# Strided-and-local attention with a squared-ReLU MLP: matmul slots of the two layers grouped by fours (by threes in the second chunk), with one head's scores ahead of the ups and one head's outputs ahead of the downs

## The chip, the cores and the metric

The kernel runs on one core of one Trainium2 chip. The metric is the device time of one execution in microseconds (us). The kernel before takes 880.53 us (median of 3 runs, 880.10 to 881.49).

## What is computed

```python
def _attn_ref(q, k, v):                       # 8 batches, 8 heads, 576 positions, 64 per head
    scores = scale * np.matmul(q, k.transpose(0, 1, 3, 2))
    rel = pos[:, None] - pos[None, :]
    mask_local = (rel >= 0) & (rel < 32)
    mask_strided = (rel >= 0) & (pos[None, :] % 32 == pos[:, None] % 32)
    # heads 0 to 3 use mask_local, heads 4 to 7 mask_strided
    attn = softmax(np.where(mask, scores, -1e9))
    return np.matmul(attn, v)

def _moe_ref(x, w_in, w_out):                 # x: 4608 tokens x 512, w_in 512 x 2048, w_out 2048 x 512
    h = np.maximum(x @ w_in, 0.0)
    return h * h @ w_out
```

The attention output of all heads, laid side by side, is the `x` of the second function. All data are float32.

## The kernel before

**Chunks and slots.** The 4608 tokens are cut into 12 chunks (`NCHUNK`) of 384 tokens (`TC`). The MLP of one chunk is 16 slots (`NFT`), one for each 128 columns of the inner dimension. Every number is split into a high and a low part, so each product is three matmuls. `up(c, j)` (L466) is the first layer of slot j: 12 matmuls of 384 columns into one PSUM bank (`psum` 0, 1 or 2, in turn), then ReLU and square on ScalarE (L487, L488; in the first chunk ReLU on ScalarE and the square on VectorE), the high part `gh` (ScalarE, L489) and the low part `gl` (VectorE, L490). `gh` and `gl` have two buffers each. `down(c, j)` (L494) is the second layer of the slot: 9 matmuls of 512 columns, three for each of the three 128-token tiles `y` of the chunk, which sum up in three banks of their own over all 16 slots. After slot 15 the three tiles are copied to `ysb` (L513) and stored (L514), all on SyncE's queue.

**Attention of the next chunk, beside the MLP of this one.** The strided heads (`strided`, L400) run on GpSimd (products, L426 and L448) and VectorE (sums over them, L427 and L449) and write `xsh`/`xsl` (L459, L460). The local heads of the first two chunks are computed in pairs (`pe_pair`, L295), those of the third and later ones (`NPLAIN`) one at a time by the generator `pe_head` (L199). It has six steps: the two loads on SyncE's queue (L214, L215), the high and low parts of q and k (L220 to L223), the four score matmuls (L237) with mask and minimum on VectorE, the softmax (L246 to L254), the transposes and `px` (L257 to L272), the four output matmuls (L283) with the writing of `xlh`/`xll` (L290, L291). Chunk c+1 has 4 such heads, 40 in all.

**What orders the work.** The framework schedules the instructions of each engine by a simulation, earlier-written ones first where several are ready; `tc.issue_after(ins)` adds that what is written in its block follows `ins` on the same engine. On TensorE this is a hand-written order: `last["pe"]` is the last instruction placed, and `take` (L580) puts the next step of a head behind it. In the first chunk (L657 to L664) ups and downs are free against each other, and the weights, loaded and split into high and low parts by `convert` (L147), come in beside them. From the second chunk on the loop (L655) goes by pairs of slots: two ups, then the two downs of the pair before. So the downs run two slots behind, and the last pair's downs of a chunk come after the first two ups of the next chunk. The table `plan` (L569) says for each of the 8 pairs which heads take a step ahead of the ups, between ups and downs, and after them: scores stand between in pairs 0 and 1 and ahead of the ups in pairs 4 and 5; outputs stand between in pairs 2 and 3 and ahead of the ups in pairs 6 and 7. The strided steps are spread over the slots by `SPREAD` and a cost count (L690 to L710).

Of the kernel before, what the change touches and what calls it, by code (L numbers as in the profile page):

```python
# [18 lines left out]
STR = 32  # L19
# [26 lines left out]
WRATE = 2  # L46

# [39 lines left out]
def attn_moe(ctx: ExitStack, tc, qk_l, v_l, qk_d, v_d, qk_p, v_p, f_s, q_s, k_s, v_s, w_in, w_out, masks, eye, out):  # L87
# [4 lines left out]
    xpool = pool("xpool", 2)  # L92
    gpool = pool("gpool", 2)
    ypool = pool("ypool", 3)
# [4 lines left out]
    ps_y = pool("ps_y", NTT, space=PSUM)  # L99
    ps = pool("ps", 1, space=PSUM)  # L100

    def psum(i, nm):
# [96 lines left out]
    def pe_head(c, h):  # L199
# [95 lines left out]
    def pe_pair(c, pr, local, qk, vr, es, pt, banks, sm, single):  # L295
# [67 lines left out]
        yield  # L363
        p4 = pt.rearrange("p (h w q) -> p h w q", h=2, w=NW)
        for h in range(2):
            t = s_ps[h] if s_ps else banks()

            for w in [*range(NW)] * (2 if c == 0 and local and not pr and h else 1):
                nc.tensor.transpose(t[:kw, w * QC : (w + 1) * QC], e4[h][:, w], ident[:QC, :QC])  # L369
            if c == 0 and not local:  # L370
                nc.vector.tensor_copy(pt[:kw, h * TC : (h + 1) * TC], t[:kw, :TC])
            else:
                last["a"] = nc.scalar.copy(pt[:kw, h * TC : (h + 1) * TC], t[:kw, :TC])
        yield
        x = x_tiles(c)
        if local:
            o = s_ps[0] if s_ps else banks()

            for w in [*range(NW)] * (3 if c == 0 and not pr else 1):
                for h in range(2):  # L380
                    nc.tensor.matmul(o[D * h : D * (h + 1), w * QC : (w + 1) * QC], v4[:kw, h, w], p4[:kw, h, w], start=True, stop=True)  # L381
            outs = [(o[:, :TC], [x["l", s][:, pr, :] for s in "hl"])]
        else:
# [3 lines left out]
            for a in range(2):  # L387
                o = s_ps[a]
                for w in range(NW):
                    for h in range(2):  # L390
                        p0 = r0 + STR * h
                        nc.tensor.matmul(o[p0 : p0 + STR, w * QC : (w + 1) * QC], v4[:kw, h, w, STR * a : STR * (a + 1)], p4[:kw, h, w], start=True, stop=True)
                by_i = lambda t: t[r0 : r0 + D].rearrange("p (s i r) -> p s i r", s=2, r=STR)
# [72 lines left out]
    def up(c, j):  # L466
# [4 lines left out]
        for kt in range(4):  # L471
# [3 lines left out]
            for w, xx in ((wi[p][0], xh), (wi[p][0], xl), (wi[p][1], xh)):  # L475
                done = nc.tensor.matmul(ph[:, :TC], w[:, wsl], xx, start=n == 0, stop=n == 11)  # L476
# [16 lines left out]

    def down(c, j):  # L494
        gh, gl = g_tiles.pop((c, j))
        p, o = divmod(j, 2)
# [8 lines left out]
        wsl = slice(o * DM, (o + 1) * DM)  # L505
        for t in range(NTT):
            sl = slice(t * P, (t + 1) * P)
            for k, (g, w) in enumerate(((gh, wo[p][0]), (gh, wo[p][1]), (gl, wo[p][0]))):
                done = nc.tensor.matmul(y_ps[c][t], g[:, sl], w[:, wsl], start=j == 0 and k == 0, stop=j == NFT - 1 and k == 2)  # L509
        if j == NFT - 1:  # L510
            for t in range(NTT):
                y = ypool.tile([P, DM], F32, name=f"ysb{c}_{t}", tag="ysb")
                (nc.scalar.copy if t == 1 else nc.vector.tensor_copy)(y, y_ps[c][t])  # L513
                nc.sync.dma_start(out=out[c * TC + t * P : c * TC + (t + 1) * P, :], in_=y)  # L514
        return done
# [17 lines left out]


    def pair_at(c, pr, local, place, psum_at):
        u = f"{c}_{pr}_{int(local)}"
        buf = lambda pl, nm, n, tag, **kw: pl.tile([P, n], F32, name=f"{nm}{u}", tag=tag, **kw)
        ee = lambda pl, tag: [buf(pl, f"e{h}", 512, tag) for h in range(2)]
        if place == 0:
            b = buf(lraw, "qk", TC + KC, "qk"), buf(lpool, "v", 512, "vx", bufs=1), ee(lpool, "e"), buf(lpool, "pt", 2 * TC, "px")  # L540
        elif place == 1:
            b = buf(lraw, "qk", TC + KC, "qk"), buf(ypool, "v", 512, "ysb"), ee(ypool, "ysb"), buf(lpool, "pt", 2 * TC, "px")
        elif place == 2:
            e = buf(xpool, "e", 2 * TC, "xlh")
            b = buf(xpool, "qk", 2 * TC, "xll"), buf(xpool, "v", 2 * TC, "xsl")[:, :512], [e[:, :TC], e[:, TC:]], buf(lpool, "pt", 2 * KC, "kx", bufs=1)[:, : 2 * TC]
        else:

            t = buf(wpool, "w", 2048, "w7")
            b = buf(xpool, "qk", 2 * TC, "xsh"), buf(spool, "v", 512, "s3", bufs=5), [t[:, :512], t[:, 512:1024]], t[:, 1024 : 1024 + 2 * TC]
        it = iter(range(10))  # L550
# [9 lines left out]
    def local(c):  # L560
# [7 lines left out]
    heads = {}  # L568
    plan = {  # L569
        0: ("", "0", "01"),  # L570
        1: ("", "1", "012"),
        2: ("", "0", "123"),
        3: ("", "1", ""),
        4: ("2", "", "23"),
        5: ("3", "", "23"),
        6: ("2", "", "3"),
        7: ("3", "", ""),
    }
# [74 lines left out]

    NS = NCHUNK * NFT
    for s in range(NS + 2):  # L655
        c, j = divmod(s, NFT)
        if s < NFT:  # L657

            with ExitStack() as seq:
                if s:  # L660
                    seq.enter_context(tc.issue_after(last["up"].ins))
                last["up"] = up(c, j)
            if s >= 2:
                last["pe"] = down(*divmod(s - 2, NFT))  # L664

        elif s % 2 == 0:
            before, between, rest = plan[j // 2]
            for part, slots, two in (up, (s, s + 1), before), (down, (s - 2, s - 1), between):
                take(c + 1, two)
                with tc.issue_after(last["pe"].ins):  # L670
                    for i in slots:
                        if 0 <= i < NS:
                            last["mm"] = part(*divmod(i, NFT))
                last["pe"] = last["mm"]
            take(c + 1, rest)
        if s < NFT - 2:

            weights = behind({"a": last["gh"]} | ({"x": last["xs"]} if s > NFT - 4 else {}), ungated)
            for _ in range(WRATE):
                next(weights, "end")  # L680
            weights_end = {e: last[e] for e in "agsv"}
        if s == LATER:
            zbank = (4,)
        if s == NFT - 1:
            with tc.issue_after(weights_end["g"].ins):
                for t in p_t:
                    nc.gpsimd.memset(t, 0.0)
        if j == NFT - 2:
            take(c + 2, "010")
        if c + 1 < NCHUNK and s >= LATER:  # L690
            j0 = LATER if c == 0 else 0
# [16 lines left out]
            if j == NFT - 1:  # L708
                run(lo)
                run(st)  # L710


# [74 lines left out]
```

## Time and profile before

| | |
|---|---|
| median of 3 runs | 880.53 us (880.10, 880.53, 881.49) |
| span of the profiled execution, first to last instruction | 877.8 us; no other time is listed for it |
| VectorE, ScalarE, GpSimd busy | 640.3, 571.4, 672.2 us (73%, 65%, 77%) |
| instructions | 14,934 |

The span is 2.7 us under the median: the rest lies before the first and after the last instruction. In the rows of the profile PE is TensorE's matmuls, PEld its weight loads, DVE VectorE, ACT ScalarE, POOL GpSimd, SPq SyncE's queue. A row of the chain of waits gives start, length and work; a row of the groups gives busy time and mean ns of one after the bar, then the idle time before it and what ended it. In a row of instructions in order of time, the start and the length come first, and an idle time before it stands in brackets. Matmuls overlap in the records: one of 512 columns is listed with 0.39 us and the next starts 0.23 us after it.

### The profile page before, as it was taken

What the parts mean: (1) busy time and instruction counts of PE and PEld (TensorE: products, weight loads), DVE (VectorE), ACT (ScalarE), POOL (GpSimd) and SP (SyncE); (2) the same over time, 40 slices, a digit from 0 to 9 for tenths busy, and PEclk for the clock granted to TensorE, in tenths of its full rate; (3) what the DMA queues carried; (4) which work ended last, traced back from release to release, by engine and by line L of the source; (5) the groups of instructions that cost most, each with busy time, mean ns of one, the idle gap of its engine ahead of it and who ended that gap; (6) DMA issues with size and microseconds to landing.
All of it is one profiled execution on the core that took longest, in us unless ns stands there. A gap on an engine that the chain in (4) does not pass through costs nothing.

```text
span 877.8 us, 14934 instructions
## 1 busy us (share of the span) xinstructions
PE 867.9 (99%) x4787; PEld 788.9 (90%) x4787; DVE 640.3 (73%) x1900; ACT 571.4 (65%) x1506; POOL 672.2 (77%) x718
## 2 busy tenths in 40 slices
PE   8999999999999999999999999999999999999997
PEld 7788899999999999999989898989898989999996
DVE  5796587797787887878878779878778787883111
ACT  6998776586576666657756758657666665664332
POOL 3689778877978989888988978996998899782000
PEclk9999999999999999999999999999999999999999
DMA  9963531223123023112102302312031021000000
GB/s 351 363 212 95 178 95 46 85 84 114 32 86 103 27 89 103 44 62 87 58 9 80 116 13 77 100 32 75 31 103 58 29 71 62 7 0 15 23 1 37
DMA packets 26799, 71.42 MB, mean 81 GB/s; under 512 B 2976, under 2 KB 8736, under 8 KB 25184
## 3 DMA queue, kind: packets, MB, share of 16 engines
q1 hardware_dynamic: 26432, 70.14, 24.1%
q8 instruction: 38, 0.62, 0.3%
q14 instruction: 41, 0.34, 0.1%
q10 hardware_dynamic: 288, 0.33, 0.1%
HBM read 61.01 MB, written 9.44 MB: 80 GB/s over the span
## 4 chain that ended last, share of the span: by engine, by line
PE 95%; ACT 2%; POOL 1%; issue 0%; DVE 0%; DVEq 0%; POOLq 0%; ACTq 0%
PE h L476 45%; PE y L509 45%; PE s L237 2%; PE o L283 2%; ACT b L353 1%; PE w_ps L606 1%; PE b L325 1%; POOL w L173 1%; ACT raw L154 0%; ACT z L166 0%; POOL pq L426 0%; ACT w L172 0%; PE b L381 0%; ACT xsh L396 0%; PE b L369 0%
## 5 line engine op out<-in xcount | busy, mean ns | idle before, releaser
L509 PE MATMUL y<-w,gh 128*128 128x512 f32 x1152 | 357.9, 391 | 0.5 <-POOL w L173 0.5
L509 PEld LDWEIGHTS y<-w,gh 128*128 128x128 f32 x1152 | 212.7, 188 | 40.5 <-POOL w L173 0.8
L476 PE MATMUL h<-xlh,w 128*128 128x384 f32 x768 | 229.1, 339 | 1.3 <-ACT xlh L396 0.6
L448 POOL TENSOR_TENSOR pp<-vs,sc 128x448 f32<-128x448 f32 (+10 forms) x192 | 190.0, 1014 | 48.8 <-DVE qs L449 23.0
L476 PE MATMUL h<-xsh,w 128*128 128x384 f32 x768 | 226.4, 335 | 0.3 <-POOL w L173 0.3
L509 PE MATMUL y<-w,gl 128*128 128x512 f32 x576 | 225.2, 392 | 0.0
L426 POOL TENSOR_TENSOR pq<-ks,qs 128x512 f32<-128x512 f32 (+2 forms) x192 | 197.7, 1050 | 18.8 <-DVE sc L427 13.3
L490 DVE TENSOR_TENSOR gl<-h,gh 128x384 fp32r<-128x384 f32 x192 | 105.5, 550 | 80.9 <-ACT gh L489 79.8
L489 ACT CAST gh<-h 128x384 fp32r<-128x384 f32 x192 | 91.8, 478 | 104.3 <-PE y L509 103.3
L487 ACT ACTIVATE h<-h 128x384 f32<-128x384 f32 x176 | 83.1, 472 | 109.8 <-PE h L476 109.3
L427 DVE TENSOR_REDUCE sc<-pq 128x8 f32<-128x512 f32 (+4 forms) x228 | 119.7, 534 | 45.1 <-POOL pq L426 41.9
L476 PEld LDWEIGHTS h<-xlh,w 128*128 128x128 f32 x768 | 141.3, 188 | 4.9 <-ACT w L172 0.9
L476 PEld LDWEIGHTS h<-xsh,w 128*128 128x128 f32 x768 | 141.3, 188 | 1.1 <-POOL w L173 0.6
L476 PE MATMUL h<-xll,w 128*128 128x384 f32 x384 | 129.0, 336 | 0.0
L509 PEld LDWEIGHTS y<-w,gl 128*128 128x128 f32 x576 | 108.1, 188 | 22.9
L476 PE MATMUL h<-xsl,w 128*128 128x384 f32 x384 | 128.4, 334 | 0.0
L449 DVE TENSOR_REDUCE qs<-pp 128x64 f32<-128x448 f32 (+11 forms) x192 | 106.4, 562 | 27.3 <-POOL pp L448 25.5
L488 ACT ACTIVATE h<-h 128x384 f32<-128x384 f32 x176 | 83.3, 473 | 3.6
L262 DVE STREAM_TRANSPOSE p_t<-e 32x128 f32<-32x128 f32 x240 | 72.3, 301 | 11.2 <-ACT e L251 6.6
L476 PEld LDWEIGHTS h<-xll,w 128*128 128x128 f32 x384 | 72.2, 188 | 2.4 <-DVE xll L397 0.3
L476 PEld LDWEIGHTS h<-xsl,w 128*128 128x128 f32 x384 | 72.1, 188 | 0.2
L246 ACT ACTIVATE e<-e,nm 96x128 f32<-96x128 f32 x160 | 62.5, 392 | 10.1 <-DVE nm L229 8.7
(101 smaller groups left out, 1076.7 us busy)
## 6 DMA issues: line engine op xcount, KB each, us to landing
qk<-qk_l SPq DMA_DIRECT2D x24, 400.0 KB, 3.2
y<-ysb SPq DMA_DIRECT2D x36, 256.0 KB, 3.5
raw<-w_in SPq DMA_DIRECT2D x7, 1024.0 KB, 10.9
qk<-qk_l SPq DMA_DIRECT2D x16, 416.0 KB, 3.6
vs<-v_s SPq DMA_DIRECT2D x10, 576.0 KB, 3.9
raw<-w_out SPq DMA_DIRECT2D x5, 1024.0 KB, 12.6
v<-v_l SPq DMA_DIRECT2D x40, 128.0 KB, 2.1
ks<-k_s SPq DMA_DIRECT2D x8, 576.0 KB, 3.8
```

The costliest lines, as they stand in the source:

```text
L246: nc.scalar.activation(e[:QC, cut(w)], e[:QC, cut(w)], AF.Exp, bias=nmax[:QC, w : w + 1], scale=-1.0, accum_out=ssum[:QC, w, :1])
L262: nc.vector.transpose(out=pt[STR * k : STR * (k + 1), :, STR * r : STR * (r + 1)], in_=e.rearrange("p (w k) -> p w k", k=KW)[STR * r : STR ...
L426: nc.gpsimd.tensor_mul(pv, kt[:, a : a + m, :], qt[:, i - i0 : i - i0 + 1, :].broadcast_to([P, m, D]))
L427: nc.vector.tensor_reduce(out=sc[:, i - i0, a : a + m], in_=pv, op=ALU.add, axis=AX.X)
L448: nc.gpsimd.tensor_mul(pv, vt[:, a : a + nd, :n], sc[:, il : il + 1, :n].broadcast_to([P, nd, n]))
L449: nc.vector.tensor_reduce(out=ot[:, il, a : a + nd], in_=pv, op=ALU.add, axis=AX.X)
L476: done = nc.tensor.matmul(ph[:, :TC], w[:, wsl], xx, start=n == 0, stop=n == 11)
L487: nc.scalar.activation(g, g, AF.Relu)
L488: nc.scalar.activation(g, g, AF.Square)
L489: last["gh"] = nc.scalar.copy(gh, g)
L490: nc.vector.tensor_sub(gl, g, f32(gh))
L509: done = nc.tensor.matmul(y_ps[c][t], g[:, sl], w[:, wsl], start=j == 0 and k == 0, stop=j == NFT - 1 and k == 2)
```

## The change

Chunks from the second on are cut into groups of slots: 3, 3, 3, 3, 4 in the second chunk (`GROUPS`), four fours in the later ones. A group is all its ups, then all its own downs, so downs no longer trail by a pair, and the first chunk's last two downs come ahead of the second chunk's first up. `plan` is gone. With n the running number of the group, head n has its scores ahead of the ups of group n and its outputs ahead of the downs of group n+1; a new `yield` makes `px` a step of its own, taken ahead of the ups of group n+1. A head's loads are asked for at the end of group n-2.

The buffers of `gh` and `gl` go from two to three pairs (two are used in the first chunk). For it `px` goes from two buffers to one, and the second pair of local heads of the first chunks keeps its transposed scores in the third pair of `g`; the transposed scores become two tiles, one for each head.

In the last group of the last chunk the downs of slot 12 come first, then those of slots 13 to 15 tile by tile. The last tile is copied out in halves by VectorE and ScalarE, and each half is stored by a queue of its own (SyncE's and ScalarE's).

```diff
+GROUPS = (3, 3, 3, 3, 4), (4, 4, 4, 4)
...
-    gpool = pool("gpool", 2)
+    gpool = pool("gpool", 1)
...
+    g_pair = lambda i, dtype=F32R: [gpool.tile([P, TC], dtype, name=f"g{i}{k}", tag=f"g{i}{k}") for k in "hl"]
...
+        yield
         src = pt.rearrange("p w q -> p (w q)")
-        px = lpool.tile([P, 2, TC], F32R, name=f"px{u}", tag="px")
+        px = lpool.tile([P, 2, TC], F32R, name=f"px{u}", tag="px", bufs=1)
...
-        gh = gpool.tile([P, TC], F32R, name=f"gh{c}_{j}", tag="gh")
-        gl = gpool.tile([P, TC], F32R, name=f"gl{c}_{j}", tag="gl")
+        gh, gl = g_pair(j % 2 if c == 0 else (c * NFT + j) % 3)
...
-    def down(c, j):
+    def down(c, j, tiles=range(NTT)):
...
+                if c == NCHUNK - 1 and t == NTT - 1:
+                    half = slice(0, DM // 2), slice(DM // 2, DM)
+                    nc.vector.tensor_copy(y[:, half[0]], y_ps[c][t][:, half[0]])
+                    nc.scalar.copy(y[:, half[1]], y_ps[c][t][:, half[1]])
+                    nc.sync.dma_start(out=rows[:, half[0]], in_=y[:, half[0]])
+                    nc.scalar.dma_start(out=rows[:, half[1]], in_=y[:, half[1]])
...
+    def on_pe(parts):
+
+        with tc.issue_after(last["pe"].ins):
+            for part, *which in parts:
+                pe = part(*which)
+        last["pe"] = pe
...
+            for i in (NFT - 2, NFT - 1):
+                on_pe([(down, 0, i)])
...
+    def head(n):
+
+        if n >= 0:
+            take(NPLAIN + n // HL, (n % HL,))
+
+    n = 0
+    for c in range(1, NCHUNK):
+        j = 0
+        for size in GROUPS[min(c, 2) - 1]:
+            slots = range(j, j + size)
+            head(n)
+            head(n - 1)
+            on_pe([(up, c, i) for i in slots])
+            head(n)
+            head(n - 1)
+            for i in slots[: size // 2]:
+                pace(c, i)
+            if slots[-1] == NFT - 1 and c == NCHUNK - 1:
+                on_pe([(down, c, slots[0])])
+                for t in range(NTT):
+                    on_pe([(down, c, i, (t,)) for i in slots[1:]])
+            else:
+                on_pe([(down, c, i) for i in slots])
+            for i in slots[size // 2 :]:
+                pace(c, i)
+            head(n)
+            head(n + 1)
+            head(n + 2)
+            n += 1
+            j += size
```

More of the change, by code (lines that the diff above doesn't have):

```diff
@@ L363, in pe_pair @@
         yield
[L364 removed]
+        p3 = [t.rearrange("p (w q) -> p w q", w=NW) for t in pt]
         for h in range(2):
@@ L492, in up @@
         return done
-    def down(c, j):
-        gh, gl = g_tiles.pop((c, j))
+    def down(c, j, tiles=range(NTT)):
+        gh, gl = g_tiles.pop((c, j)) if tiles[-1] == NTT - 1 else g_tiles[c, j]
         p, o = divmod(j, 2)
@@ L505, in down @@
         wsl = slice(o * DM, (o + 1) * DM)
-        for t in range(NTT):
+        for t in tiles:
             sl = slice(t * P, (t + 1) * P)
@@ L652, in attn_moe, with pace @@
     zbank = (3, 4)
[L654 to L690, printed above, removed]
+    def pace(c, j):
+        nonlocal lo, st, dl, ds, cost
+        if c + 1 < NCHUNK and (c or j >= LATER):
             j0 = LATER if c == 0 else 0
@@ L710, in attn_moe @@
                 run(st)
+    lo = st = dl = ds = cost = None
+    for j in range(NFT):
+        with ExitStack() as seq:
+            if j:
+                seq.enter_context(tc.issue_after(last["up"].ins))
+            last["up"] = up(0, j)
+        if j >= 2:
+            last["pe"] = down(0, j - 2)
+        if j < NFT - 2:
+            weights = behind({"a": last["gh"]} | ({"x": last["xs"]} if j > NFT - 4 else {}), ungated)
+            for _ in range(WRATE):
+                next(weights, "end")
+            weights_end = {e: last[e] for e in "agsv"}
+        if j == LATER:
+            zbank = (4,)
+        if j == NFT - 1:
+            with tc.issue_after(weights_end["g"].ins):
+                for t in p_t:
+                    nc.gpsimd.memset(t, 0.0)
+            for i in (NFT - 2, NFT - 1):
+                on_pe([(down, 0, i)])
+        if j == NFT - 2:
+            take(2, "010")
+        pace(0, j)
+    def head(n):
[17 more added lines that the diff above has]
+                    on_pe([(down, c, i, (t,)) for i in slots[1:]])
+            else:
+                on_pe([(down, c, i) for i in slots])
[6 more added lines that the diff above has]
+            j += size
 _NAMES = ["qk_l", "v_l", "qk_d", "v_d", "qk_p", "v_p", "f_s", "q_s", "k_s", "v_s", "w_in", "w_out", "masks", "eye"]
```

35 lines of the change are left out of this document (14 added, 21 removed).

## The prediction

> **What bounds the kernel now.** I read the page first, for the engine that has no idle time.
>
> ```profile
> span 877.8 us, 14934 instructions
> PE 867.9 (99%) x4787; PEld 788.9 (90%) x4787; DVE 640.3 (73%) x1900; ACT 571.4 (65%) x1506; POOL 672.2 (77%) x718
> PEclk9999999999999999999999999999999999999999
> ```
>
> TensorE is busy 867.9 of 877.8 us at full granted clock. So only three things can move the time: how closely its matmuls follow each other, a place where they halt, and what lies before the first and after the last. The chain of waits, in order of time, shows the first of these.
>
> ```profile
> by line: PE h L476 44.9%; PE y L509 44.8%; PE s L237 2.2%; PE o L283 1.9%; ACT b L353 0.7%; PE w_ps L606 0.6%; PE b L325 0.6%; POOL w L173 0.6%; issue 0.4%; ACT raw L154 0.4%; ACT z L166 0.3%; POOL pq L426 0.2%; ACT w L172 0.2%; PE b L381 0
> ...
> 172.05 4.19 PE h L476 x24
> ...
> 382.25 4.19 PE h L476 x24
> 386.91 4.13 PE y L509 x18
> ...
> 399.82 4.19 PE h L476 x24
> 404.44 4.11 PE y L509 x18
> ...
> 417.74 4.16 PE h L476 x24
> 421.90 4.13 PE y L509 x18
> ...
> 435.21 4.21 PE h L476 x24
> ...
> 452.30 4.19 PE h L476 x24
> ...
> 802.57 4.18 PE h L476 x24
> 806.75 4.12 PE y L509 x18
> ```
>
> Ups, downs, scores and outputs are 94% of the chain, and a chunk is 452.30 - 382.25 = 70.05 us. Within it there is no wait, but the same work has several lengths. 24 ups take 4.16 right behind a head's scores (417.74), 4.19 behind downs, 4.21 behind outputs. The gaps between pieces are heads: 386.91 - 386.44 = 0.47 for the scores, 404.44 - 404.01 = 0.43 for the outputs. The kinds change 16 times in a chunk, besides the heads.
>
> The tail, in order of time, gives the speed of downs without a change of kind, and what follows the last matmul.
>
> ```profile
> 868.86 1.52 PE L509 MATMUL y<-w,gh 128*128 128x512 f32 x6
> 872.26 0.84 PE L509 MATMUL y<-w,gl 128*128 128x512 f32 x3
> 872.69 1.29 DVE L513 COPY ysb<-y 128x512 f32<-128x512 f32 x2 [2.74 <-PE y L509]
> 873.41 1.31 SPq L514 DMA_DIRECT2D y<-ysb  x3
> ```
>
> Six downs span 1.52 of which the last is 0.39, so one starts every 1.13/5 = 0.226 us, and 18 take 4.07 against 4.11 to 4.13 where they follow something else.
>
> **The change part by part.**
>
> *Regrouping, chunks 3 to 11.* Matmuls are the same in number and kind; only their neighbours change. A group of four is scores 0.47, 24 ups behind scores 4.16, 24 more behind ups 4.16, outputs 0.43, 18 downs behind outputs 4.11, 18 behind downs 4.07: 17.40. Four make 69.60, against 70.05: 0.45 less for each of nine chunks, 4.05 us. All of it is on TensorE and thus on the path.
>
> *Chunk 2.* It begins now at the wait at 105.96 (below) and chunk 3's ups begin at 172.05. After: 16 slots of ups 33.28, of downs 32.54 and five switches of about 0.04, five scores 2.35, four outputs 1.72, 70.1 in all, so 176.06. By then the two downs that now trail (4.12) and one score more (0.47) are done as well, so the like point of before is 176.64: gain 0.6.
>
> *Chunk 12* has no heads. Now 802.57 to 873.10, less the trailing downs of chunk 11 (4.12): 66.41. After: 4 x (4.18 + 4.16 + 4.12 + 4.07) = 66.12: gain 0.3.
>
> *From chunk 1 to 2.* Matmuls, then GpSimd, in order of time:
>
> ```profile
> 99.54 0.39 PE L509 MATMUL y<-w,gl 128*128 128x512 f32 x1
> ...
> 100.93 0.88 PE L381 MATMUL b<-pt,v 128*64 128x96 f32 x16
> 102.39 0.62 PE L476 MATMUL h<-xlh,w 128*128 128x384 f32 x2 [0.58 <-ACT xlh L396]
> ...
> 105.96 0.71 PE L237 MATMUL s<-kx,qx 128*96 128x256 f32 x4
> ```
>
> ```profile
> 102.41 1.30 POOL L173 TENSOR_TENSOR w<-raw,w 128x512 fp32r<-128x512 f32 x1
> ...
> 104.89 1.01 POOL L223 TENSOR_TENSOR qx<-qk,qx 64x384 fp32r<-64x384 f32 x1
> ```
>
> Chunk 2's first ups halt before 102.39 for `xlh`. With the last downs of chunk 1 put first, that halt is covered: from 99.77, 0.88 for L381 and 4.1 for two downs make 104.8. But next come the scores of the first head, which need `qx`, ready at 105.90. They start at 105.96 now and would again, with 18 downs done in place of 24 ups (4.1 against 4.2). So I take 0: the halt moves from `xlh` to `qx`. If GpSimd takes L173 and the parts of k and q before its wait that ends at 101.45, up to 1.2 is gained; a longer refill after the halt may cost 0.3.
>
> *Steps at no cost.* `px` with one buffer: it is written ahead of ups, after the last head's outputs of the group before. Halved `pt`, borrowed `g`: no instruction more. The head's two loads stay 40 each on SyncE's queue, now a group (17 us) before their use:
>
> ```profile
> qk<-qk_l SPq DMA_DIRECT2D x24, 400.0 KB, 3.2
> ```
>
> They land in 3.2 us, and uncovered would cost that once a head. Copies of `y` get 8 us of ups before the next downs, where they have 4 now.
>
> *The end.* Stores of the last three tiles, then a copy of 256 columns from PSUM:
>
> ```profile
> L514 SPq DMA_DIRECT2D y<-ysb x3: 333/383/412, 873.4 to 874.3; - x3
> ...
> DMA to landing us min/median/max: 2.1/2.3/2.5
> ```
>
> ```profile
> L241 DVE TENSOR_TENSOR e<-s,mask_sb 96x256 f32<-96x256 f32 x80 | 31.3, 412 | 11.2 <-PE s L237 10.9
> ```
>
> Now the last store is issued at 874.3, 1.2 after the last matmul (873.10), and lands 2.3 later. After: 0.19 to the copy, 0.41 for a half, 0.1 to the issue, 2.3: 3.0 in place of 3.5. The other tiles end 4.1 and 2.0 us earlier and no longer queue ahead. Gain 0.5, between 0.3 (ScalarE's queue slower) and 0.9 (landing faster with a third of the bytes).
>
> *The price: a bank inside a group of four.* Ups have three banks, so the fourth up of a group waits until the first is squared, copied and split. From the groups:
>
> ```profile
> L490 DVE TENSOR_TENSOR gl<-h,gh 128x384 fp32r<-128x384 f32 x192 | 105.5, 550 | 80.9 <-ACT gh L489 79.8
> L489 ACT CAST gh<-h 128x384 fp32r<-128x384 f32 x192 | 91.8, 478 | 104.3 <-PE y L509 103.3
> L487 ACT ACTIVATE h<-h 128x384 f32<-128x384 f32 x176 | 83.1, 472 | 109.8 <-PE h L476 109.3
> ```
>
> Undisturbed, that is 0.47 + 0.47 + 0.48 + 0.55 = 1.97 us. The first up ends 2.24 after its start, the fourth starts at 6.24: 4.0 us, so 2.0 to spare. Queued behind a halted fourth up is all of TensorE. The trace of before never has this wait, since the banks wait for downs anyway (103.3 us of ScalarE's idle time), but it shows ScalarE and VectorE put other work between:
>
> ```profile
> 246.34 0.47 ACT L487 ACTIVATE h<-h 128x384 f32<-128x384 f32 x1 [0.90 <-PE h L476]
> 246.81 0.57 ACT L220 CAST kx<-qk 128x448 fp32r<-128x448 f32 x1
> 247.28 0.51 ACT L222 CAST qx<-qk 128x384 fp32r<-128x384 f32 x1
> 247.70 0.47 ACT L488 ACTIVATE h<-h 128x384 f32<-128x384 f32 x1
> ...
> 249.64 0.46 ACT L489 CAST gh<-h 128x384 fp32r<-128x384 f32 x1
> ```
>
> ```profile
> 250.24 0.54 DVE L490 TENSOR_TENSOR gl<-h,gh 128x384 fp32r<-128x384 f32 x1
> ```
>
> Here it took 246.34 to 250.78, 4.44 us, 0.5 too long. Part of that is the wait for a `g` buffer, which the first slot of a group no longer has, its buffer having been read a group before. And the casts of k and q are ready as soon as the scores are done, 2 us before the first up ends. So I expect most groups within 4.0 us and a few over, on average 0.02 us (0.2 in one group of ten) for the 1 + 36 + 4 = 41 groups of four: 0.8 us. Ends: 0, and 0.5 x 41 = 20. I am near the low end because of the 2.0 us to spare.
>
> Sum: 4.05 + 0.6 + 0.3 + 0 + 0.5 - 0.8 = 4.65 us off the span of 877.8. The median lies 2.7 above the span, which I leave: 880.53 - 4.65 = **875.9 us**.
>
> [...]
>
> **The rivals.**
>
> *Slower: the fourth up halts in nearly every group.* The exponentials of the head follow the scores, hence fall right on the first slot's square and copy. At 0.3 us for each of 41 groups it costs 12.3 against a gain of 5.4: 887.4 us. From 0.13 us a group nothing is left (5.4/41), from 0.17 it is slower by 0.2%. For it: the 4.44 above. Against it: 2.0 to spare, and ScalarE is idle a third of the time. Chance 0.16.
>
> *The regrouping brings nothing of itself.* The long first matmuls after a change would then belong to what the other engines do just then, and be met again elsewhere; with the end alone the time is 880.5 - 0.5 = 880.0. Against it: 4.19 and 4.16 stand by what precedes them. Chance 0.10. [...]
>
> *Halts of 0.09 to 0.17 us a group* cost 3.7 to 7.0 of the gain of 5.4: 878.8 to 882.1. Chance 0.08.
>
> *Both open places fall well.* No bank wait, GpSimd's order shifts (1.2) and the end gives 0.9: 880.5 - 4.95 - 1.2 - 0.9 = 873.5. Chance 0.12.
>
> *Strided work late.* GpSimd writes the last chunk's `xsl` only just in time:
>
> ```profile
> 794.97 1.84 POOL L460 TENSOR_TENSOR xsl<-ks,xsh 128x768 fp32r<-128x768 f32 x1 [2.64 <-ACT xsh L459]
> ```
>
> It ends at 796.81, 5.8 before chunk 12 (802.57). After, chunk 12 begins at 873.10 - 4.95 - 66.1 = 802.05, because the trailing downs now come first: 5.2 remain. It decides only if GpSimd slips by over 5 us, and then takes what is beyond; at 8 us of slip the gain is halved, 878.7. Chance 0.04.
>
> That the order is not what is written is hardly possible, as each part is put behind the one before on TensorE.
>
> **How the numbers follow.** A difference under about 0.2% (1.8 us) can't be told from none. The forecast, 874.5 to 878.0, has 0.50. Faster by over 0.2% (under 878.8): forecast 0.50, both places well 0.12, strided work 0.04: 0.66. Within: regrouping nothing 0.10, smaller halts 0.08: 0.18. Slower: 0.16. The range is 873.2 to 882.3: below, the good case; above, to where the slower rival begins, which is left out.
>
> **What would show it.** Right: ups of a group as 48 without a gap at 8.3 us, chunks of 69.6, scores of the first head again near 105.9 behind a wait for `qx`, and 3.0 us from the last matmul to the last landing. Wrong: an idle time on PE h that VectorE's `gl` ends, in the fourth up; a gap at a chunk's start ended by `xsl` or `xll`; or switches of over 0.05 us between groups.

## The result and the profile after

| | before | after |
|---|---|---|
| median of 5 runs | 880.53 us (880.10 to 881.49) | **915.15 us** (913.59 to 917.09) |
| span of the profiled execution | 877.8 us | 913.7 us |

The ratio is 1.0394 (95% 1.0383 to 1.0406). The kernel became 34.6 us slower. The forecast was 4.6 us faster, and 915.15 lies far above the range. The head of the page of after:

```profile
span 913.7 us, 14796 instructions
PE 877.6 (96%) x4787; PEld 792.4 (87%) x4787; DVE 637.6 (70%) x1900; ACT 562.3 (62%) x1507; POOL 672.6 (74%) x718
```

TensorE ran the same 4787 matmuls, but it is now idle for 36 us of the span in place of 10, and busy 9.7 us longer. The other three engines are no busier than before, so the time did not go into more work anywhere. In after, the up matmuls are line 481, `gh` and `gl` 493 and 494, downs 513, scores 241 and outputs 288; heads have their exponentials at 250, multiplications at 255 and transposes at 266. The view of waits gives, for TensorE, the line that waited, what it waited for, us in total, times, and the longest:

```profile
PE h L481 <- DVE g1l L494: 11.4, 6, 3.8
PE h L481 <- DVE g0l L494: 9.3, 6, 3.2
PE h L481 <- DVE g2l L494: 3.4, 5, 0.8
...
PE y L513 <- POOL w L177: 1.5, 2, 1.0
...
PE s L241 <- POOL qx L227: 0.5, 1, 0.5
```

24.1 us are waits of ups for a `gl`, that is for a bank. The view lists 17 of them. Worked out from the starts of matmuls (the fourth up's first less the third up's last, less the 0.17 us at which such matmuls follow each other), the halts at fourth ups sum to **27.8 us over the 41 groups of four**, 0.68 each. No such halt falls in chunk 12, whose groups have no heads beside them.

Where a group has no halt, it went as forecast. From the chain of waits, a group of chunk 9 (start, length, work):

```profile
649.80 8.32 PE h L481 x48
658.12 0.42 PE o L288 x4
658.54 8.20 PE y L513 x36
666.74 0.47 PE s L241 x4
667.21 8.32 PE h L481 x48
```

One group takes 667.21 - 649.80 = 17.41 us; the forecast was 17.40.

What a halt is made of shows in one group of chunk 5. TensorE, in order of time, the third up's last matmul and the fourth's first:

```profile
397.73 0.34 PE L481 MATMUL h<-xsh,w 128*128 128x384 f32 x1
400.62 0.69 PE L481 MATMUL h<-xlh,w 128*128 128x384 f32 x1 [2.55 <-DVE g1l L494]
401.10 0.53 PE L481 MATMUL h<-xll,w 128*128 128x384 f32 x1
```

The group's first up had its last matmul done at 393.90. ScalarE, from then on:

```profile
395.02 0.19 ACT L250 ACTIVATION_READ_ACCUMULATOR e<-e,nm 96x1 f32 x1
395.11 0.47 ACT L491 ACTIVATE h<-h 128x384 f32<-128x384 f32 x1
395.61 0.47 ACT L492 ACTIVATE h<-h 128x384 f32<-128x384 f32 x1
396.00 0.97 ACT L255 ACTIVATE e<-e,rs 96x128 f32<-96x128 f32 x3
...
397.58 0.46 ACT L493 CAST g1h<-h 128x384 fp32r<-128x384 f32 x1
```

And VectorE:

```profile
398.11 1.87 DVE L266 STREAM_TRANSPOSE p_t<-e 32x128 f32<-32x128 f32 x6
400.00 0.56 DVE L494 TENSOR_TENSOR g1l<-h,g1h 128x384 fp32r<-128x384 f32 x1
```

The four steps that free the bank need 1.97 us undisturbed. Here they take 6.66 (393.90 to 400.56). ReLU stands behind the exponentials and starts 1.2 us late, `gh` behind multiplications and the next slot's ReLU (square over at 396.08, `gh` at 397.58: 1.5 us), and `gl` behind six transposes (`gh` over at 398.04, `gl` at 400.00: 2.0 us). Over all groups of four the way from the first up's end to the end of its `gl` takes 4.19 us on average, 7.9 at most, and 2.1 in chunk 12. TensorE allows 4.0.

Not every group looks like this one. 20 of the 41 groups halt for more than 0.05 us. In seven of these the multiplications and transposes stand ahead of the first slot's casts, as here; these seven halts are the longest and sum to 19.0 of the 27.8 us. In the other 13 (8.8 us) the exponentials stand ahead, and in most of them sums of the strided heads (lines 432 and 454).

The halts cost more than themselves. The windows view of the same place gives busy us (and count) of TensorE, its weight loads, VectorE, ScalarE and GpSimd, then the granted clock: before the halt, in it, after it.

```profile
391.60:397.90 6.30, 6.30 (x38) 6.15 (x36) 4.54 (x18) 5.68 (x19) 6.14 (x8) 1.00 0.21 65
397.90:400.60 2.70, 0.17 (x1) 0.00 (x0) 2.60 (x9) 2.14 (x6) 1.63 (x2) 0.92 0.00 0
400.60:403.40 2.80, 2.78 (x9) 2.78 (x10) 2.51 (x6) 0.00 (x0) 2.30 (x3) 0.50 0.00 0
```

Behind the halt the clock was granted at 0.50, and nine matmuls took 2.78 us, where 16 go at 0.17 us apart. Together with the longer first spacing behind the shorter halts (0.28 us in place of 0.17, called the refill below), this added 8.9 us, worked out as the time by which matmuls behind halts overrun their usual spacing.

The end, in order of time:

```profile
909.09 0.42 DVE L520 COPY ysb<-y 128x256 f32<-128x256 f32 x1 [3.39 <-PE y L513]
909.54 0.33 SPq L522 DMA_DIRECT2D y<-ysb  x1
909.55 0.37 ACT L521 COPY ysb<-y 128x256 f32<-128x256 f32 x1 [1.91 <-DVE ysb L520]
909.95 0.35 ACTq L523 DMA_DIRECT2D y<-ysb  x1
```

ScalarE's half does not run beside VectorE's. It starts when VectorE's is done (idle until `DVE ysb L520`), so the second store is issued 0.9 after the last matmul's end (909.05), and the span ends 913.7 - 909.05 = 4.65 after it, against 4.70 before.

### The profile page after: what moved, and what is told of

Same layout as the page of the kernel before. It is cut to its first block, busy times and chain, and to the rows that moved or that the text cites. A ratio compares the mean times of both kernels' runs of the same rounds, so it can differ in the third digit from the quotient of the medians.

```text
span 913.7 us, 14796 instructions
## 1 busy us (share of the span) xinstructions
PE 877.6 (96%) x4787; PEld 792.4 (87%) x4787; DVE 637.6 (70%) x1900; ACT 562.3 (62%) x1507; POOL 672.6 (74%) x718
## 4 chain that ended last, share of the span: by engine, by line
PE 57%; POOL 17%; DVE 13%; ACT 7%; issue 4%; DMA 1%; POOLq 0%; DVEq 0%; ACTq 0%
PE y L513 30%; PE h L481 24%; POOL pp L453 6%; POOL pq L431 4%; DVE p_t L266 3%; POOL w L177 2%; POOL qx L227 2%; DVE qs L454 2%; DVE sc L432 1%; PE o L288 1%; POOL kx L225 1%; PE s L241 1%; ACT e L250 1%; DMA raw<-w_out 1%; DVE e L245 1%
## 5 line engine op out<-in xcount | busy, mean ns | idle before, releaser
L481 PE MATMUL h<-xlh,w 128*128 128x384 f32 x768 | 233.5, 345 | 25.3 <-DVE g1l L494 11.4
L481 PEld LDWEIGHTS h<-xlh,w 128*128 128x128 f32 x768 | 143.9, 191 | 33.8 <-DVE g1l L494 14.1
L432 DVE TENSOR_REDUCE sc<-pq 128x8 f32<-128x512 f32 (+4 forms) x228 | 119.7, 534 | 58.6 <-POOL pq L431 53.5
L481 PEld LDWEIGHTS h<-xsh,w 128*128 128x128 f32 x768 | 143.4, 190 | 1.2 <-POOL w L177 0.7
L454 DVE TENSOR_REDUCE qs<-pp 128x64 f32<-128x448 f32 (+11 forms) x192 | 107.2, 563 | 45.4 <-POOL pp L453 44.2
L513 PE MATMUL y<-w,g1h 128*128 128x512 f32 x402 | 114.9, 392 | 1.5 <-POOL w L177 1.5
L513 PE MATMUL y<-w,g0h 128*128 128x512 f32 x396 | 113.5, 391 | 0.0
L513 PE MATMUL y<-w,g2h 128*128 128x512 f32 x354 | 100.3, 390 | 0.0
L224 ACT CAST kx<-qk 128x416 fp32r<-128x416 f32 (+1 forms) x40 | 22.1, 552 | 113.5 <-PE s L241 78.5
L513 PEld LDWEIGHTS y<-w,g1h 128*128 128x128 f32 x402 | 74.2, 188 | 16.6 <-POOL w L177 2.2
L513 PEld LDWEIGHTS y<-w,g0h 128*128 128x128 f32 x396 | 73.3, 188 | 14.1 <-ACT g0h L493 0.3
L513 PEld LDWEIGHTS y<-w,g2h 128*128 128x128 f32 x354 | 65.6, 188 | 12.8
```

Of the source, the lines that this page charges most:

```text
L224: nc.scalar.copy(kx[:, 0, :nk], kr[:, :nk])
L432: nc.vector.tensor_reduce(out=sc[:, i - i0, a : a + m], in_=pv, op=ALU.add, axis=AX.X)
L454: nc.vector.tensor_reduce(out=ot[:, il, a : a + nd], in_=pv, op=ALU.add, axis=AX.X)
```

## The experiments

The theory after this result: the halts come from the order of work on ScalarE and VectorE. A head's softmax and transposes become ready during the first two ups of its group, and stand in the queues ahead of the casts that free the first bank. Rivals were a shortage of banks as such, GpSimd's strided products, for which VectorE's sums wait (53.5 us at L432 and 44.2 at L454 in the page of after), and the size of the groups. Every kernel below is after with an edit, whose main lines are shown; the last one is before with an edit. Line numbers shift by a few between them; the comments in the diffs are added for the reader. The framework makes the order of each engine anew for every kernel, so an edit also moves instructions that it does not name.

**Leave out part of a head's work (k2_no_transpose).**

```diff
-            for w in range(NW):            # multiplications
+            for w in range(0):
...
-        for r in range(QC // STR):         # transposes
+        for r in range(0):
```

> The changed kernel with the head's multiplications by 1/sum on ScalarE (three heads of four) and its six transposes on VectorE left out. Theory: the long halts all had the transposes ahead of gl, so the halts fall under 8 us, time 876 to 888 us. Rival A (sums waiting for GpSimd): halts over 18 us, time over 895 us.

One run took 879.18 us, span 877.2, and the halts sum to 2.3 us. The waits of ups for a bank in it:

```profile
PE h L481 <- DVE g0l L494: 0.5, 2, 0.3
```

Without these two kinds of instruction nearly all of the halts are gone. They stand ahead of the first `gl` in the seven groups with 19.0 us; most of the other 8.8 us went as well, from groups in which the two did not stand ahead in after. The new order may account for that; it was not taken apart. The kernel leaves work out, so it shows who is in the way and not what a sound version would take.

**Leave out the strided heads' work (k1_no_strided).**

```diff
-            for i in range(i0, i1):
+            for i in range(i0, i1 if c < 2 else i0):     # both loops of products and sums
```

> The changed kernel with the strided heads' products and sums left out from the third chunk on (GpSimd and VectorE do neither; the rest of that path stays). It takes away every wait of VectorE for GpSimd's products and a good third of VectorE's work. Theory (the head's own work stands ahead of gl): halts of the fourth up stay over 12 of 27.8 us, time over 890 us. Rival A (sums waiting for GpSimd): halts under 4 us, time 876 to 880 us.

One run took 922.65 us, span 920.9. The halts grew to 36.0 us:

```profile
PE h L481 <- DVE g1l L494: 12.6, 7, 3.8
PE h L481 <- DVE g0l L494: 11.5, 7, 3.2
PE h L481 <- DVE g2l L494: 8.6, 6, 1.7
```

GpSimd's products and VectorE's sums are therefore not the main thing that holds the banks, and that rival falls as the main cause. The trace also shows why the halts grew: in the new order the multiplications and transposes stand ahead of the first `gl` in 18 groups in place of seven, and these 18 hold 28.6 of the 36.0 us, most of them 1.55 each. Of the other 23 groups 21 have no halt. In the two that have one (7.3 us together) VectorE first waits 4.65 and 4.08 us for a load of the strided heads. Since groups with the exponentials alone ahead do not halt here, the sums of the strided heads probably have a part in the 8.8 us that after lost in its 13 groups; no run separates that part.

**Put softmax and transposes behind the first slot's casts (e1_behind).** `evac` keeps the `gh` and `gl` of each slot, and a head's steps are queued behind them on their engines.

```diff
-        nc.vector.tensor_sub(gl, g, f32(gh))
+        evac[c, j] = last["gh"], nc.vector.tensor_sub(gl, g, f32(gh))
...
-    def head(n):
+    def head(n, after=()):
+        with ExitStack() as st:
+            for i in after:
+                st.enter_context(tc.issue_after(i.ins))
...
-            head(n)                        # softmax; transposes
+            head(n, evac[c, j])
```

> The changed kernel, but a head's softmax and its transposes are queued on ScalarE and VectorE behind the first slot's gh and gl of the same group; all else as it is. Theory: the loss is the fourth up of a group of four halting for its PSUM bank (27.8 us of halts in 41 groups, and some 8 us of slow clock behind the longest), because the head's exponentials, multiplications and transposes stand ahead of the first slot's gh and gl in the queues. Then the halts fall under 5 us and the time to 876 to 884 us. Rival A, VectorE's sums that wait for GpSimd's products hold gl back: the sums stay where they are, so the halts stay over 15 us and the time over 898 us. Rival B, the group is too full and a wait only moves: halts at other places (outputs, scores, downs) of over 10 us, time over 890 us.

It took 894.54 us (893.56 to 895.80) against 879.90; ratio 1.0164 (1.0147 to 1.0181). The fourth ups' halts fell from 27.8 to 5.1 us, as the theory wants, but the time came out over ten us above what I expected:

```profile
PE h L481 <- ACT xsh L464: 2.4, 1, 2.4
PE h L481 <- DVE g0l L494: 1.9, 1, 1.9
...
PE y L513 <- DVE g2l L494: 1.6, 3, 0.7
...
PE h L481 <- POOL xsl L465: 1.5, 1, 1.5
PE y L513 <- ACT g2h L493: 1.4, 1, 1.4
```

As the rival B of its forecast had it, the waits changed their place: downs of chunk 2's threes now wait for the casts of later slots, and one chunk's strided `xsh` and `xsl` came late. Behind the first slot's casts the head's work is still ahead of the next slots'.

**Put them behind the last slot's casts (e10_late_only).** The same edit with one index changed, and nothing else: three banks, start and end as in after.

```diff
-            head(n)                        # softmax; transposes
+            head(n, evac[c, slots[-1]])
```

> The changed kernel with one thing altered: a head's softmax and transposes are queued on ScalarE and VectorE behind the gh and gl of the last slot of its group. Three banks, the start of the second chunk and the end stay as the change has them. Theory: the order of the head's ScalarE and VectorE work is the cause, so the halts of the fourth up fall from 27.8 to under 4 us and the time to 875 to 880 us; the fourth bank adds little. Rival (the bank is needed: what is left ahead of gl, px and the sums of the strided heads, still holds the fourth up): halts over 8 us, 883 us and over.

It took **876.85 us** (876.29 to 877.53) against 880.38; ratio 0.9957 (0.9944 to 0.9971). The halts are down to 0.44 us in all, and the bank is free 2.58 us after the first up on average. The same place as above, VectorE in order of time:

```profile
395.54 0.56 DVE L494 TENSOR_TENSOR g1l<-h,g1h 128x384 fp32r<-128x384 f32 x1
...
402.38 1.87 DVE L266 STREAM_TRANSPOSE p_t<-e 32x128 f32<-32x128 f32 x6
```

The transposes now run in the middle of the downs (396.49 to 404.68 in its chain of waits), where no bank is waited for. This pair, after and e10, shows the cause: all engines run the same instructions, and TensorE's ups, downs, scores and outputs follow each other in the same order (within a piece, 305 of its 4787 matmuls change places). The edit sets the order on ScalarE and VectorE alone and takes 38.3 us away; GpSimd's order, which the framework made anew, changed with it. The strided sums are all in place in e10, so they do not hold the banks once the head's work is out of the way.

**A fourth bank for the fourth up (e7_fourth_bank).** The second half of a head's outputs goes to the first up's bank in return.

```diff
-        ph = psum((c * NFT + j) % 3, f"h{c}_{j}")
+        ph = psum(at[c, j] if c else j % 3, f"h{c}_{j}")
...
+            at |= {(c, i): (0, 1, 2, 4)[i - j] for i in slots}
...
-            return psum(3 + next(turn) % 2, f"{nm}{u}")
+            return psum({"s0": 3, "s2": 4, "o0": 3, "o2": 0}[nm], f"{nm}{u}")
```

> The changed kernel with a fourth bank for the fourth up: it takes one of the heads' two, free by then, and the second half of a head's outputs goes to the first up's bank. Order, groups and buffers stay. It takes away the wait for the first slot's gl at the fourth up; the downs ask for that gl only 6.7 us after its up's end. Theory: the halts fall from 27.8 to under 4 us and no slow clock is left, 875 to 880 us. Rival (the head's work delays gl so far that the downs halt in place of the up): halts over 10 us, time over 888 us.

It took 887.09 us (886.51 to 887.32) against 880.27; ratio 1.0077 (1.0064 to 1.0090). Fourth ups halt 0.02 us in all, but the outputs, which stand next, wait for the same late casts, since their second half now uses the first up's bank:

```profile
PE o L288 <- DVE g1l L494: 5.0, 3, 2.4
PE o L288 <- DVE g0l L494: 1.9, 3, 0.9
```

The time lies between the two forecasts, and neither names the place of these waits. The way from the first up's end to `gl` is no shorter than in after (4.59 us against 4.19). A bank more takes 28.1 of the 34.6 us away, so the shared bank is a condition of most of the loss. It does not take the late casts away, and what is left is their wait at the next reader.

**No groups of four at all (e5_threes).**

```diff
-GROUPS = (3, 3, 3, 3, 4), (4, 4, 4, 4)
+GROUPS = (3, 3, 3, 3, 2, 2), (3, 3, 3, 3, 2, 2)
```

Heads keep to the first groups of a chunk.

> The changed kernel with no group of four: 3, 3, 3, 3, 2, 2 in every chunk, a head in each of the first five groups of the second chunk and of the first four of the later ones; scores and outputs stay ahead of ups and downs. No up shares a bank within its group. Theory: the first slot's gl comes 4.2 us on average after its up's end (7.9 at most), and the downs of a group of three ask for it 4.4 us after, so the halts go from the fourth up to the first downs: 8 to 20 us of them, time 886 to 898 us. Rival (the shared bank alone is the trouble, gl is early enough for all else): halts under 3 us, time 876 to 879 us.

It took 908.45 us (907.51 to 908.59) against 880.27; ratio 1.0319 (1.0305 to 1.0333), 10 us above the upper end of what I expected. The time falls by only 6.7 us, since now the downs, which follow two ups after the first, wait for the casts of their own group.

```profile
PE y L513 <- DVE g1l L494: 4.1, 6, 1.0
PE y L513 <- ACT g1h L493: 3.1, 1, 3.1
PE y L513 <- DVE g2l L494: 3.0, 8, 0.7
PE y L513 <- DVE g0l L494: 2.8, 5, 0.8
```

So smaller groups take the shared bank away and do not cure the loss: by the forecast's figures their downs ask for the first `gl` 4.4 us after its up's end, those of a four 6.7 us after. In before the downs ran a pair behind their ups, and the 4.44 us that the prediction quotes halted nobody.

**Scores ahead of the downs, outputs ahead of the ups, two groups on (e3_shift).** The head's work then falls into other stretches.

```diff
-            head(n)                        # scores
-            head(n - 1)                    # px
+            head(n - 2)                    # outputs
             on_pe([(up, c, i) for i in slots])
-            head(n)
-            head(n - 1)                    # outputs
+            head(n - 1)
+            head(n)                        # scores
...
             head(n)                        # softmax
+            head(n - 1)                    # px
```

> The changed kernel, but scores stand ahead of the downs of group n and outputs ahead of the ups of group n+2, so that a head's softmax falls on the downs; the second chunk has groups of 3, 3, 3, 3, 2, 2. Groups of four stay. Theory: with the softmax off the first slot's path the halts of the fourth up fall under 8 us, time 876 to 886 us. Rival A (sums that wait for GpSimd): halts over 15 us, time over 895 us. Rival B: halts at the outputs or scores take their place, time over 890 us.

It took 880.32 us (878.57 to 881.62) against 879.90; ratio 1.000 (0.999 to 1.0009). Fourth ups halt 1.0 us in all: moving the head on TensorE cures the halts too. But ups behind outputs and downs behind scores cost 0.05 us each, a group takes 17.48 us, and only about 0.15 us a chunk is won; some 4 us of halts and longer spacings between 102 and 190 us remained. A second version (**e6_shift_b**) takes the start of chunk 2 as before (chunk 1's last two downs behind chunk 2's first ups), groups it 2, 3, 3, 3, 3, 2, and copies the last tile whole with ScalarE:

```diff
-                    nc.vector.tensor_copy(y[:, half[0]], y_ps[c][t][:, half[0]])
-                    nc.scalar.copy(y[:, half[1]], y_ps[c][t][:, half[1]])
+                    nc.scalar.copy(y, y_ps[c][t])
+                    nc.sync.dma_start(out=rows, in_=y)
```

> The kernel with scores ahead of downs and outputs ahead of ups two groups on, with the first chunk's last two downs put back behind the second chunk's first ups (as in the kernel before), groups of 2, 3, 3, 3, 3, 2 in the second chunk, and the last tile copied whole by ScalarE and stored once. That kernel took 880.3 us, with some 4 us of halts between 102 and 190 us, and none later. Theory: these go with the start of the second chunk, and the regrouping is worth what was forecast (0.4 us a chunk): 875 to 878.5 us. Rival (the second chunk is full, halts come back elsewhere in it): 879 us and over.

It took 879.62 us (878.77 to 880.91) against 880.27; ratio 0.9994 (0.9985 to 1.0003), no difference that can be told. That is outside the forecast and in the range of its rival; its trace has halts of 0.4 to 0.6 us (at 102.3, 173.3 and 177.5), again around chunk 2.

**Everything that helped, together (e8_late_soft).** Softmax and transposes behind the last slot's casts as in e10, four banks as in e7, start and end as in e6.

```diff
+            if not n:                      # behind chunk 2's first ups
+                on_pe([(down, 0, i) for i in (NFT - 2, NFT - 1)])
+                head(n)
+            head(n, evac[c, slots[-1]])
```

> The kernel with the fourth bank (887.1 us), with a head's softmax and transposes queued on ScalarE and VectorE behind the gh and gl of the last slot of its group, so that they fall on the downs; the first chunk's last two downs are back behind the second chunk's first ups, and the last tile is copied whole by ScalarE and stored once. Scores stay ahead of ups, outputs ahead of downs. Theory: the regrouping and the placing are worth what was forecast once the head's ScalarE and VectorE work is off the ups: halts under 2 us from the second chunk on, 873.5 to 877 us. Rival (the head's chain is now too short of time, px and the outputs come late, or the strided work does, as where the softmax was queued behind the first slot): halts over 6 us, 880 us and over.

It took **874.32 us** (874.15 to 875.68) against 880.48; ratio 0.9935 (0.9923 to 0.9947), the fastest here and faster than both kernels of the change. The head of its page:

```profile
span 872.5 us, 14854 instructions
PE 863.8 (99%) x4787; PEld 786.9 (90%) x4787; DVE 640.6 (73%) x1899; ACT 580.1 (66%) x1507; POOL 673.8 (77%) x718
```

A group stays at 17.42 us (663.86 - 646.44 in its chain), and no halt is left from the second chunk on. The last matmul ends at 868.42; the sum of the prediction without the allowance for halts puts it at 873.10 - 4.95 = 868.15. The match is in part luck: the first up of all starts at 25.73 here and at 26.05 in before, and over the 13 traces it starts between 25.50 and 27.26. The end:

```profile
868.46 0.58 ACT L519 COPY ysb<-y 128x512 f32<-128x512 f32 x1 [1.45 <-PE y L513]
869.07 0.33 SPq L520 DMA_DIRECT2D y<-ysb  x1
```

One copy of 0.58 us by ScalarE is shorter than the two halves in a row (0.42 and 0.37 with a hand-over), and the last store is issued 0.65 after the last matmul in place of 0.90. Yet the span ends 4.1 us after the last matmul, where it ends 3.63 after it with the halves of e11: in e3, whose trace has both, a whole tile's store landed 2.0 us after its issue, the halves' 1.7. Against e10 the span is 3.3 us shorter. Of this, 0.8 lies ahead of the first up (25.73 against 26.56), in work that the edits leave alone; 1.4 more comes by chunk 3's first up (175.83 against 178.09), where e10 waits 1.4 for L177 in the downs and 0.5 for `qx` in the scores and e8 0.5 and nothing; 0.85 comes in chunks 3 to 11, with 0.44 of fourth-up halts; and 0.1 at the end.

**The same, one slot earlier (e9_late_soft2):** `evac[c, slots[-2]]`.

> The same, but queued behind the last slot but one, so that the softmax need not wait for the g buffer that the last slot waits for. Theory: as above, 873.5 to 877 us, and within 1 us of it. Rival (the softmax again delays the last slot's gh and gl): halts at the downs of over 5 us, 879 us and over.

It took 878.28 us (876.72 to 879.15) against 880.48; ratio 0.9971 (0.9960 to 0.9982). That is outside the forecast, and the halts are fewer than its rival had. Even one slot ahead of the last, the head's work delays downs:

```profile
PE y L513 <- DVE g0l L494: 1.0, 2, 0.5
```

These are downs of chunk 2, where a group of three leaves the last casts the least time. Of the 4.0 us by which the last matmul ends after that of e8, 2.7 arise in chunk 2. The other 1.3 stand ahead of its first up, in the profiled execution at least, whose mean granted clock is 0.997 where the other six have 1.0.

**The end alone (e11_tail).** Before, with the change's order of the last downs and its halves.

```diff
+                if part is down and slots[1] == NS - 1:
+                    for t in range(NTT):
+                        with tc.issue_after(last["pe"].ins):
+                            for i in slots:
+                                last["pe"] = down(*divmod(i, NFT), (t,))
+                    continue
```

> The kernel before with the change's end alone: the last pair's downs tile by tile, the last tile copied out in halves by VectorE and ScalarE, two queues for its stores. Forecast: 0.5 us less (0.3 to 0.9) if the halves are copied side by side; if ScalarE's half waits for VectorE's (as the changed kernel's profile shows), the store of the second half is issued 0.85 us after the last matmul, and the gain is 0.2 to 0.6 us from the other tiles' earlier stores alone. Either lies near what can be told from none: 879.5 to 880.3 us beside 880.5.

It took 880.21 us (878.18 to 880.86) against 880.38; ratio 0.9996 (0.9987 to 1.0005). The halves again run one after the other (0.42 from 875.06, 0.37 from 875.52). Yet the span ends 3.63 us after the last matmul (875.02), against 4.70 in before: 1.1 less in the traces. The medians can't tell it, since executions differ by as much elsewhere: in this one chunk 3's first up starts 1.8 later than in before's (173.69 against 171.89), ahead of anything that the edit touches.

## Why the prediction was wrong

**The step that failed** is "The price: a bank inside a group of four". It set "most groups within 4.0 us and a few over, on average 0.02 us", 0.8 us in all. Measured were 27.8 us of halts (0.68 a group) and 8.9 us of slow or refilling matmuls behind them. The 4.44 us that the prediction quoted (from the ReLU's start) for one of "a few over" is near the mean of after, 4.19 (from the up's end). Four things went wrong in it:

- It measured the slack with the undisturbed 1.97 us and took for granted that ScalarE and VectorE would get to the casts when these are ready. The change itself puts a head's scores right ahead of a group's ups, so that the exponentials, multiplications and transposes come ready within the very 4.0 us in question. The row of the transposes (1.87 us) was never put against the 2.0 us to spare. With that alone the spare time was gone.
- It misread the 4.44 us. "Part of that is the wait for a `g` buffer" is not in the trace of before. ScalarE has no idle time ahead of that `gh`; the head's four exponentials stand there, from 248.11 to 249.64, 1.5 us, in rows that the prediction's excerpt skips (below).
- "ScalarE is idle a third of the time" is a share of the whole run. In the group shown the stretch that counts was full: 5.68 of 6.30 us busy in the window ahead of the halt.
- Its sum counted a halt at its own length. Behind each of the five halts with a slow clock, the clock and the refill cost some 1.5 us more.

The first and the last of the four exponentials in the trace of before:

```profile
248.11 0.38 ACT L246 ACTIVATE e<-e,nm 96x128 f32<-96x128 f32 x1
...
249.26 0.39 ACT L246 ACTIVATE e<-e,nm 96x128 f32<-96x128 f32 x1
```

**The rival** "the fourth up halts in nearly every group" named this mechanism and its place. It was given 0.16, and priced at 0.3 us a group, 12.3. By the runs it should have been 0.68 + 8.9/41 = 0.90, 36.7 us. It was wrong on how often: 20 of the 41 groups halt, and seven of them make up two thirds.

**Regrouping** (4.05 + 0.6 + 0.3) was right: 17.41 us a group against 17.40 forecast, 69.65 a chunk against 69.60, and the last matmul ends within 0.3 us of the forecast sum once the halts are gone (e8, with some luck, as said there). The rival that regrouping brings nothing falls with it: the groups of e10 and e8 take 17.41 and 17.42 us on the chip with every engine's work in them. **From chunk 1 to 2** was put at 0; the scores started at 106.53 instead of 105.96, so it cost 0.6. They waited for `qx`, as forecast, but GpSimd's wait ahead of its parts ended at 102.03 instead of 101.45, and the two downs put first waited 1.0 for a weight (L177). Late or stretched downs in chunk 2's threes cost another 1.7, which no step had. **The end** was put at 0.5, between 0.3 and 0.9. It had the copies side by side and the last store issued 0.70 after the last matmul; they do not overlap, and it is issued at 0.90 (1.20 in before). From the last matmul to the span's end there are 4.70 us in before and 4.65 in the profiled execution of after, where the last two stores took 2.9 and 2.8 us to land. In seven of the nine traces with this end, e11 among them, there are 3.63 to 3.88, with landings of 1.7 in e3 and k2 (2.1 to 2.5 in before), and 4.2 in e10. So the step is worth about 1 us by most traces, by a faster landing more than by the copies, and after's 0.05 is one execution.

**Strided work late** did not occur in after, whose chunk 12 has no halt; in e1 it did once (2.4 and 1.5 us).

The sum for the last matmul: forecast without allowance 868.15, measured 909.05, 40.9 more. Of this 27.8 are halts of fourth ups, 8.9 slow or refilling matmuls, 1.7 downs of chunk 2, and 0.6 its start: 39.0. The remaining 1.9 stay open. The prediction also added 2.7 us from the span to the median as time outside the span. The later runs list both: an execution of before with the same span of 877.8 took 879.60 us, 1.8 more, so the profiled execution was some 0.9 us quicker than the median. The forecast difference does not hang on it.

**The clock.** In after 0.50 was granted behind the halt at 397.9, but only five of the 20 halts were followed by slow matmuls. Behind the other 15 (0.84 us on average) the first spacing alone was longer, 0.28 us in place of 0.17. The longest wait that the view lists for TensorE in before is 1.6 us, and the mean granted clock there is 0.999, so that trace did not show this cost.

What stays open besides: what part the sums of the strided heads have in the 8.8 us of halts without transposes ahead.

## What to carry to other kernels

A buffer's slack is not its free time less the bare latency of the steps that free it; it is what is left after everything that becomes ready in the same stretch on the same engines, and the change's own reordering decides what that is. When a matmul engine is full, place the side work of ScalarE and VectorE explicitly behind the instructions that free its banks: here that one order was worth 38 us. One more bank was worth 28 and smaller groups 7, and both left the wait to the next reader. Ask of each regrouping which lag (here a pair of slots between up and down) had been hiding late casts.

## What the hardware showed beside

The length of a halt alone does not say in this run whether the clock drops. From the start of the last matmul before it to the start of the first behind it, the six longest halts of after take 4.16, 3.58, 2.98, 2.89, 2.50 and 2.39 us. Behind five of them seven or eight matmuls in a row started 0.32 us apart in place of 0.17. Behind the one of 2.50 none did, though the one of 2.39 was shorter.

The clock records of after list five drops to 0.50 while TensorE had work, from 171.47, 212.43, 325.07, 400.16 and 546.94, each 3.41 us long. Here are the 3.41 us ahead of the drop at 400.16, the drop itself, the halt of 2.50 and what came behind it; the first figures are the length and TensorE's busy time, the third last is the granted clock:

```profile
396.75:400.16 3.41, 1.32 (x8) 1.00 (x6) 2.88 (x9) 3.29 (x9) 2.78 (x3) 1.00 0.12 49
400.16:403.57 3.41, 2.95 (x9) 2.95 (x10) 3.12 (x7) 0.00 (x0) 2.47 (x3) 0.50 0.00 0
285.30:287.80 2.50, 0.40 (x3) 0.08 (x1) 2.36 (x8) 2.47 (x8) 0.00 (x0) 1.00 0.22 83
287.80:290.60 2.80, 2.74 (x17) 2.74 (x18) 1.88 (x9) 0.38 (x2) 1.25 (x4) 1.00 0.00 0
```

TensorE was idle for 2.09 us of the first stretch, and for 1.95 to 3.41 us of the 3.41 us ahead of each of the five drops. In the third stretch it was idle for 2.10 us, and the clock behind it was granted at 1.00. What decides whether the clock drops, no run here shows.
